# Sums for a seven-product block scheme moved to GpSimd, a ring of six tiles for the split operands, and one reordered visit

## The chip, the cores and the metric

The kernel runs on one core of a Trainium2 chip. The core has five engines that run side by side, each with its own queue of instructions taken in order: TensorE (PE, the matrix products), VectorE (DVE), ScalarE (ACT), GpSimd (POOL) and SyncE (SP, which here issues nearly all transfers). They meet at semaphores: an instruction waits at the head of its queue until what it needs is done. The metric is the device time of one execution in microseconds (us). Several executions are timed, and the median counts.

## The reference

Two things are computed one behind the other. For each of 8 batches and 8 heads, rows `x` (512 x 64) and a small state (32 x 64) attend to each other:

```python
scores = scale * x @ state.T;   a  = softmax(scores);  xread = a @ state
scores2 = scale * state @ x.T;  a2 = softmax(scores2); sread = a2 @ x
```

`xread` and `sread` of all heads make 4608 rows of 512 numbers (544 rows per batch). Each row then goes through a two-layer network with an activation that is x times the tanh of the softplus of x, called mish:

```python
h = x @ w_in                    # 512 -> 2048
g = h * np.tanh(softplus(h))
out = g @ w_out                 # 2048 -> 512
```

All is in float32.

## The kernel before

**Precision.** TensorE is run in a fast format (fp32r) that keeps fewer bits. So each operand of a large product is split in a high part (a rounded copy, `gh`) and a low part (what is left, `gl = g - gh`), and a product is three matmuls: high by high, high by low, low by high. For `g` a "unit" goes through the same steps each time: mish on ACT writes `u` (or `g`), a copy makes the high part, and a subtraction on DVE makes the low part. Then PE uses both.

**First product.** `xread` is never formed. As `xread @ w_in = a @ (state @ w_in)`, the kernel multiplies the state by a slice of `w_in` on PE (`sw_slice`, L567, output `swp`), splits the result on ACT and DVE (`swh`, `swl`), and multiplies it by the split soft-max (`ah`, `al`) in `gemm1` (L614, output `ph`). The columns of `w_in` are taken in 8 slots (`SLOTS`) of 256.

**Second product.** Batches 0 and 1 use the plain product (`second`, `gemm2`, output `acc`). From batch 2 on, blocks are multiplied by a scheme that takes seven products in place of eight: a pair of 128-row blocks by a pair of 256-column blocks, for five of the eight slots (`SEVEN = 5`); the three other slots take the plain four products of double width. The seven products need sums and differences of blocks, on both sides. Those of `w_out` are made once per slot by `seven_weights` (L891), in batch 1, slots 3 to 7. Those of `g` are made for each unit in `prepare` (L1050), in a tile `sums`, and split like `u` itself. A unit is one pair of row blocks of one slot: batch `key`, half `p` (0 or 1), slot `j`. `consume` (L1076) issues the 21 matmuls of a seven-product unit, or 12 of a plain one, to four PSUM banks (`acc_one`, `acc_two`, `acc_top`, `acc_end`), and behind the fifth unit it adds two of the banks up in `sums_{key}_{p}`.

**Order.** The main loop (L1120) takes batches 2 to 6, then the state reads (`"s"`), then batch 7. In each slot it issues: `gemm1` and mish of this slot; `one()`, a unit of the second product; `around`, which is a visit to the next batch's attention (slot 3: scores, state reads, a `sw_slice`; slot 5: a `sw_slice`; slot 7: two); `other()`, a second unit; `after` (DVE and ACT work for the next batch's soft-max, and loads); and `two_next`, which makes the parts of two more units. In batch 2 the units of the first half become ready one per slot, so `other()` has nothing to issue from slot 3 on; from batch 3 on two units are used in each slot. PE takes its instructions in the order written (`InOrder`, L56 on). From batch 1 on, DVE and ACT are ordered by a planner that works with modelled times and priorities; GpSimd is in written order. Instructions can be held behind others of the same engine (`behind`).

**Buffers.** Tiles with one tag share `bufs` places. `gh` and `gl` have two places each, of 1024 columns, so the parts of at most two units exist at a time: the high copy of the next must wait until PE has used the one two before. `g` (batches 0 and 1) has one place. Small working tiles (`temp`, five places) hold `sums` and the soft-max. A `ph` bank is one of two (`ps_h`), and a `sw_slice` in slot 7 borrows both.

Of the kernel before, what the change touches and what calls it, by code (L numbers as in the profile page):

```python
# [9 lines left out]
F32 = mybir.dt.float32  # L10
F32R = mybir.dt.float32r
# [6 lines left out]
P = 128  # L18
# [62 lines left out]
def state_attention_mish_kernel(ctx, tc, x, state, w_in, w_out, out):  # L81
# [515 lines left out]
        return gh, gl  # L597

    def new_parts(key):
        return [pool.tile([P, W], F32R, tag=t, name=f"{t}_{key}") for t in ("gh", "gl")]  # L600

    def high_g(key, g, copy=None):
        gh, gl = new_parts(key)
# [5 lines left out]
        last["low"] = dve.tensor_sub(gl, g, as_f32(gh))  # L609

    def new_g(key):
        return pool.tile([P, W], F32, tag="h", name=f"g_{key}", bufs=1)

    def gemm1(b, j, aT, sw, ks=(0, 1)):  # L614
        swh, swl = sw[j]
# [275 lines left out]
    def seven_weights(j):  # L891


        if not wx:
            wx.append(const.tile([P, SEVEN, 2, 3, 256], F32R, tag="w_in", name="wx"))
        w = pool.tile([P, 4, 256], F32, tag="wt", name=f"w_sums_{j}", bufs=1)
        dve.tensor_add(
            w.rearrange("p (k e) c -> p k (e c)", k=2), as_f32(wo[j][:, :, 0]), as_f32(wo[j][:, :, 1]))
        dve.tensor_sub(w[:, 0], w[:, 0], w[:, 1])
        dve.tensor_sub(w[:, 1], w[:, 3], w[:, 1])  # L900
        dve.scalar_tensor_tensor(w[:, 3], w[:, 3], -1.0, w[:, 0], ALU.mult, ALU.subtract)
        dve.tensor_add(w[:, 2], w[:, 2], w[:, 3])
        low, high = (wo[j][:, 0, n, 256:] for n in range(2))
        act.copy(high, w[:, 0])
        dve.tensor_sub(low, w[:, 0], as_f32(high))
        low, high = (wx[0][:, j, n] for n in range(2))
        act.copy(high, w[:, 1:])
        dve.tensor_sub(low, w[:, 1:], as_f32(high))
# [51 lines left out]
    def after(key, j):  # L960


        nonlocal sn_next
        more = key + 1 < B
        if key == 1 and j < 2:
            for g in range(2 * j, 2 * j + 2):
                nc.sync.dma_start(w_in_again[:, :, g * G:(g + 1) * G], w_in_sb[:, :, g * G:(g + 1) * G])
        if key == 1 and 3 <= j < 3 + SEVEN:
            seven_weights(j - 3)
        if key == 1 and j == 0:  # L970
            prev["soft2"]()
        if key == 1 and j == 1:
            with behind("mish"):
                prev["turn"]()
        if more and j == (0 if key == 1 else 1):
            with behind("swl"):
                for c in range(NC):
                    own["x"](c)
                own["xd"](0)
        if more and j == 1:  # L980
            with behind("swl"):
                own["st"](0)
        if more and key > 1 and j == 2:
            wis[key, 2] = load_w_in_again(2)
        if not more and j == 0:
            wis[key, 2], wis[key, 3] = load_w_in_again(2), load_w_in_again(3)
        if more and j == 3:
            with behind("swh", "swl"):
                own["soft2"]()
            if key > 1:  # L990
                wis[key, 3] = load_w_in_again(3)
        if more and j == 4:
            wis[key + 1, 0] = load_w_in_again(0)
            with behind("low before", "swh", "swl"):
                own["soft1"]()
        if more and j == 5:
            wis[key + 1, 1] = load_w_in_again(1)
            with behind("mish"):
                own["turn"]()
        if key == 1 and j == 3:  # L1000
            with behind("store"):
                xss[2] = load_x(2)
        if 1 < key < B - 1 and j == 4:
            with behind("mish"):
                xss[key + 1] = load_x(key + 1)
        if key == B - 2 and j == 6:
            with behind("mish"):
                sreads_moved()
        if more and j == 7:
            own["parts"]()  # L1010
            if key + 2 < B:
                load_x_in(key + 2)
                with behind("mish"):
                    sn_next = load_state(key + 2)
        if key == B - 2 and j == 7:
            wis["s", 0] = load_w_in_again(0, "x", 1)
            wis["s", 1] = load_w_in_again(1)
            with behind("mish", "low"):
                sreads_split()
# [30 lines left out]
    def prepare():  # L1050

        if not todo or todo[0] not in made:
            return
        unit = todo.pop(0)
        key, p, j = unit
        u = made.pop(unit).rearrange("f k h t -> f (k h) t")
        hi, lo = (pool.tile([P, 7, P], F32R, tag=t, name=f"{t}_{key}_{p}_{j}") for t in ("gh", "gl"))
        n = 3 if j < SEVEN else 4
        if j < SEVEN:
            sums = temp(f"sums_{key}_{p}_{j}").rearrange("f (s t) -> f s t", s=4)  # L1060
            dve.tensor_add(sums[:, :2], u[:, 1:3], u[:, 3:].to_broadcast([P, 2, P]))
            dve.tensor_add(sums[:, 2], sums[:, 0], u[:, 2])
            dve.tensor_add(sums[:, 3], sums[:, 2], u[:, 0])
            act.copy(hi[:, :n], u[:, :n])
            act.copy(hi[:, n:], sums)
            low_g(u[:, :n], hi[:, :n], lo[:, :n])
            low_g(sums, hi[:, n:], lo[:, n:])
        else:
            dve.tensor_copy(hi[:, :n], u)
            low_g(u, hi[:, :n], lo[:, :n])  # L1070
        parts[unit] = hi, lo
        ready.append(unit)
# [3 lines left out]
    def consume():  # L1076
# [21 lines left out]
        if j == SEVEN - 1:  # L1098
            e = spans[key, p]["sums"] = pool.tile([P, 4, 256], F32, tag="wt", name=f"sums_{key}_{p}", bufs=1)
            one, two = (banks[n].rearrange("t (h e) -> t h e", h=2) for n in ("one", "two"))  # L1100
            act.copy(e[:, 0], one[:, 0])
            dve.tensor_add(e[:, 3], e[:, 0], one[:, 1])
            dve.tensor_add(e[:, 1:3], two, e[:, 3:].to_broadcast([P, 2, 256]))
            dve.tensor_add(e[:, 3], e[:, 1], two[:, 1])

# [14 lines left out]
    for key in [*range(2, B - 1), "s", B - 1]:  # L1120
        for j in range(4 if key == "s" else SLOTS):
            one, other = halves()
            if key == "s":
                if j == 0:
                    one()
                    sread_transposed()
                    other()
                for r in range(2):
                    gemm1_s(j, r, wis["s", j], new_unit("s", 0, 2 * j + r))
                    if j:  # L1130
                        (one, other)[r]()
                if j < 2:
                    wis["s", j + 2] = load_w_in_again(j + 2, *(() if j else ("x", 1)))
            else:
                mish_units(key, j, gemm1(key, j, aTs[key], sw))
                one()
                around(key, j)
                other()
                after(key, j)
            two_next()  # L1140
# [29 lines left out]
```

## Time and profile before

| | |
|---|---|
| median of 3 runs | 662.51 us (661.88 to 664.02) |
| profiled execution | 661.25 us |
| its span in the profile | 659.5 us |
| busy in the span: PE, DVE, ACT, POOL | 633.3, 461.9, 333.3, 0.7 us |

The span is what the profile covers, from the first to the last instruction; the profiled execution's own time is 1.75 us longer. Busy time of PE counts a matmul from its start to its end, and matmuls overlap: one with 256 columns follows the one before it after some 0.12 us and one with 512 after 0.23 us, though each is shown as 0.28 or 0.39 us long. In rows of the timeline the first number is the start in the span and the second the length; rows that follow one another are merged (x2, x4). In brackets stands the idle time of the engine before the row and what ended it. Nearly all instructions carry line 73, that of the helper which records them, so they are told apart by the tile that they write and read (`gl<-u,gh`).

### The profile page before, as it was taken

What the parts mean: (1) busy time and instruction counts of PE and PEld (TensorE: products, weight loads), DVE (VectorE), ACT (ScalarE), POOL (GpSimd) and SP (SyncE); (2) the same over time, 40 slices, a digit from 0 to 9 for tenths busy, and PEclk for the clock granted to TensorE, in tenths of its full rate; (3) what the DMA queues carried; (4) which work ended last, traced back from release to release, by engine and by line L of the source; (5) the groups of instructions that cost most, each with busy time, mean ns of one, the idle gap of its engine ahead of it and who ended that gap; (6) DMA issues with size and microseconds to landing.
All of it is one profiled execution on the core that took longest, in us unless ns stands there. A gap on an engine that the chain in (4) does not pass through costs nothing.

```text
span 659.5 us, 12906 instructions
## 1 busy us (share of the span) xinstructions
PE 633.3 (96%) x5108; PEld 529.1 (80%) x5108; DVE 461.9 (70%) x951; ACT 333.3 (51%) x654; POOL 0.7 (0%) x6
## 2 busy tenths in 40 slices
PE   8999999999996899999999999999999899999997
PEld 6776777786875688797978798888888689888996
DVE  6998984799549554977398746975496787546554
ACT  5998853544346433843365444734374375343320
POOL 0000000000000000000000000000000000000000
PEclk9999999999996999999999999999999999999999
DMA  8999826412633263526263254435163441301000
GB/s 321 409 343 325 296 55 196 129 32 69 191 106 125 84 168 94 200 73 166 67 204 118 84 148 149 136 100 160 26 223 101 154 136 51 109 1 33 1 33 32
DMA packets 69035, 89.83 MB, mean 136 GB/s; under 512 B 13808, under 2 KB 42224, under 8 KB 68976
## 3 DMA queue, kind: packets, MB, share of 16 engines
q1 hardware_dynamic: 68544, 88.83, 41.9%
q8 instruction: 40, 0.66, 0.4%
q10 hardware_dynamic: 432, 0.20, 0.1%
q14 instruction: 19, 0.16, 0.1%
HBM read 63.90 MB, written 13.11 MB: 117 GB/s over the span
## 4 chain that ended last, share of the span: by engine, by line
PE 77%; DVE 10%; DMA 6%; ACT 4%; issue 2%; SPq 1%; DVEq 0%; ACTq 0%
PE ph L73 23%; PE acc_top L73 12%; PE acc L73 9%; PE acc_end L73 9%; PE acc_two L73 6%; PE acc_one L73 6%; DMA wir<-in_moe_w_in_dram 3%; PE swp L73 3%; PE ph_s L73 3%; DVE gl L73 2%; DVE sums L73 2%; DVE swl L73 1%; DMA wor<-in_moe_w_out_dram 1%; PE srp L73 1%; PE sc L73 1%
## 5 line engine op out<-in xcount | busy, mean ns | idle before, releaser
L73 ACT ACTIVATE u<-ph 128x256 f32<-128x256 f32 x192 | 63.7, 384 | 107.8 <-PE ph L73 104.0
L73 DVE TENSOR_TENSOR gl<-u,gh 128x384 fp32r<-128x384 f32 (+1 forms) x96 | 58.1, 606 | 73.7 <-ACT gh L73 72.1
L73 PE MATMUL acc_top<-wo,gh 128*128 128x256 f32 (+1 forms) x384 | 91.8, 327 | 1.0 <-DVE gh L73 1.0
L73 PE MATMUL ph<-ah,swh 128*128 128x512 f32 (+1 forms) x260 | 82.1, 396 | 8.6 <-DVE swl L73 6.4
L73 PE MATMUL ph<-ah,swl 128*128 128x512 f32 (+1 forms) x260 | 80.4, 390 | 0.0
L73 PE MATMUL ph<-al,swh 128*128 128x512 f32 (+1 forms) x260 | 80.1, 390 | 0.2 <-DVE al L73 0.2
L73 PE MATMUL acc<-wo,gh 128*128 128x512 f32 x256 | 80.0, 393 | 0.0
L73 PEld LDWEIGHTS acc_top<-wo,gh 128*128 128x128 f32 x384 | 64.0, 192 | 9.4 <-DVE srds L73 1.6
L73 ACT CAST gh<-u 128x384 fp32r<-128x384 f32 x60 | 30.9, 515 | 74.5 <-PE acc_end L73 69.0
L73 PEld LDWEIGHTS ph<-ah,swh 128*128 128x128 f32 x260 | 46.5, 189 | 22.2 <-DVE swl L73 8.6
L73 PE MATMUL acc_top<-wo,gl 128*128 128x256 f32 (+1 forms) x192 | 62.4, 325 | 0.5 <-DVE gl L73 0.5
L73 PEld LDWEIGHTS ph<-ah,swl 128*128 128x128 f32 x260 | 48.9, 189 | 11.7 <-DVE swl L73 1.2
L73 PEld LDWEIGHTS acc<-wo,gh 128*128 128x128 f32 x256 | 47.4, 188 | 12.7 <-issue 2.9
L73 PEld LDWEIGHTS ph<-al,swh 128*128 128x128 f32 x260 | 48.8, 189 | 10.9 <-DVE al L73 0.4
L73 ACT ACT_TABLE_LOAD x35 | 44.9, 1283 | 13.8 <-DVE nm L73 7.0
L73 PE MATMUL acc<-wo,gl 128*128 128x512 f32 x128 | 49.9, 390 | 0.0
L73 DVE TENSOR_TENSOR swl<-swp,swh 128x512 fp32r<-128x512 f32 (+1 forms) x72 | 42.2, 628 | 10.5 <-ACT swh L73 10.4
L73 ACT CAST swh<-swp 128x512 fp32r<-128x512 f32 (+1 forms) x72 | 34.6, 546 | 19.3 <-PE swp L73 18.7
L73 PE MATMUL acc_end<-wo,gh 128*128 128x512 f32 x144 | 44.4, 389 | 0.0
L73 DVE TENSOR_TENSOR gl<-sums,gh 128x512 fp32r<-128x512 f32 x60 | 41.5, 691 | 0.0
L73 PEld LDWEIGHTS acc_top<-wo,gl 128*128 128x128 f32 x192 | 36.8, 192 | 3.8 <-DVE gl L73 0.9
L73 ACT CAST gh<-sums 128x512 fp32r<-128x512 f32 x60 | 37.1, 618 | 4.2 <-DVE sums L73 4.2
(174 smaller groups left out, 1179.7 us busy)
## 6 DMA issues: line engine op xcount, KB each, us to landing
w_in<-w_in_again SPq DMA_DIRECT2D x28, 1024.0 KB, 6.3
x<-in_x_dram SPq DMA_DIRECT2D x32, 256.0 KB, 6.2
wir<-in_moe_w_in_dram SPq DMA_DIRECT2D x16, 512.0 KB, 10.2
wor<-in_moe_w_out_dram SPq DMA_DIRECT2D x16, 512.0 KB, 9.3
out_dram<-o SPq DMA_DIRECT2D x31, 256.0 KB, 2.6
x_rows<-x_turned SPq DMA_DIRECT2D x56, 128.0 KB, 2.4
x_in<-in_x_dram SPq DMA_DIRECT2D x24, 256.0 KB, 4.0
w_in_again<-w_in_sb SPq DMA_DIRECT2D x4, 1024.0 KB, 9.4
```

What stands on the lines that cost most here:

```text
L73: made = method(*args, **kwargs)
```

## The change

Three parts of the kernel are edited.

- `g`, `gh` and `gl`, and the two parts of a unit, all take places in one ring with the tag `"g"`, six places of 1024 columns, where there were two, two and one. A unit's parts are views of 7 x 128 columns of them.
- The sums of `w_out` blocks (five instructions for each of five slots) and the sums of `g` blocks (three for each seven-product unit) go from DVE to GpSimd. One instruction of the weights, which negated and subtracted in one step, becomes a plain addition; the sign is taken back by two subtractions, the last of the weights' five and one where the banks are added up in `consume`. `seven_weights` is now held behind the last `swl` (on DVE) and the last mish (on ACT).
- In slot 5, the sixth, `around` comes ahead of `one()`.

```diff
     def new_parts(key):
-        return [pool.tile([P, W], F32R, tag=t, name=f"{t}_{key}") for t in ("gh", "gl")]
+        return [pool.tile([P, W], F32R, tag="g", name=f"{t}_{key}", bufs=6) for t in ("gh", "gl")]
...
     def new_g(key):
-        return pool.tile([P, W], F32, tag="h", name=f"g_{key}", bufs=1)
+        return pool.tile([P, W], F32, tag="g", name=f"g_{key}", bufs=6)
...
         w = pool.tile([P, 4, 256], F32, tag="wt", name=f"w_sums_{j}", bufs=1)
-        dve.tensor_add(
+        pool_e.tensor_add(
             w.rearrange("p (k e) c -> p k (e c)", k=2), as_f32(wo[j][:, :, 0]), as_f32(wo[j][:, :, 1]))
-        dve.tensor_sub(w[:, 0], w[:, 0], w[:, 1])
-        dve.tensor_sub(w[:, 1], w[:, 3], w[:, 1])
-        dve.scalar_tensor_tensor(w[:, 3], w[:, 3], -1.0, w[:, 0], ALU.mult, ALU.subtract)
-        dve.tensor_add(w[:, 2], w[:, 2], w[:, 3])
+        pool_e.tensor_sub(w[:, 0], w[:, 0], w[:, 1])
+        pool_e.tensor_sub(w[:, 1], w[:, 3], w[:, 1])
+        pool_e.tensor_add(w[:, 3], w[:, 3], w[:, 0])
+        pool_e.tensor_sub(w[:, 2], w[:, 2], w[:, 3])
...
         if key == 1 and 3 <= j < 3 + SEVEN:
-            seven_weights(j - 3)
+            with behind("swl", "mish"):
+                seven_weights(j - 3)
...
-        hi, lo = (pool.tile([P, 7, P], F32R, tag=t, name=f"{t}_{key}_{p}_{j}") for t in ("gh", "gl"))
+        hi, lo = (
+            pool.tile([P, W], F32R, tag="g", name=f"{t}_{key}_{p}_{j}", bufs=6).rearrange("f (s t) -> f s t", t=P)
+            for t in ("gh", "gl"))
...
-            dve.tensor_add(sums[:, :2], u[:, 1:3], u[:, 3:].to_broadcast([P, 2, P]))
-            dve.tensor_add(sums[:, 2], sums[:, 0], u[:, 2])
-            dve.tensor_add(sums[:, 3], sums[:, 2], u[:, 0])
+            pool_e.tensor_add(sums[:, :2], u[:, 1:3], u[:, 3:].to_broadcast([P, 2, P]))
+            pool_e.tensor_add(sums[:, 2], sums[:, 0], u[:, 2])
+            pool_e.tensor_add(sums[:, 3], sums[:, 2], u[:, 0])
             act.copy(hi[:, :n], u[:, :n])
-            act.copy(hi[:, n:], sums)
+            act.copy(hi[:, n:7], sums)
             low_g(u[:, :n], hi[:, :n], lo[:, :n])
-            low_g(sums, hi[:, n:], lo[:, n:])
+            low_g(sums, hi[:, n:7], lo[:, n:7])
...
             act.copy(e[:, 0], one[:, 0])
-            dve.tensor_add(e[:, 3], e[:, 0], one[:, 1])
+            dve.tensor_sub(e[:, 3], e[:, 0], one[:, 1])
...
                 mish_units(key, j, gemm1(key, j, aTs[key], sw))
-                one()
+                if j != 5:
+                    one()
                 around(key, j)
+                if j == 5:
+                    one()
                 other()
                 after(key, j)
```

## The prediction

> **What bounds the kernel now.** I read the page first: the busy times, then the chain that ended last.
>
> ```profile
> span 659.5 us, 12906 instructions
> ...
> PE 633.3 (96%) x5108; PEld 529.1 (80%) x5108; DVE 461.9 (70%) x951; ACT 333.3 (51%) x654; POOL 0.7 (0%) x6
> ...
> PE 77%; DVE 10%; DMA 6%; ACT 4%; issue 2%; SPq 1%; DVEq 0%; ACTq 0%
> ```
>
> TensorE (PE) is the bound, and GpSimd (POOL) is empty. The change takes no matmul away, so it can only win time in which PE stands still: 659.5 - 633.3 = 26.2 us. The table of waits for PE, from 150 us on, says what it stood still for (total, times, longest):
>
> ```profile
> PE ph L73 <- DVE swl L73: 6.4, 5, 2.7
> PE acc_one L73 <- ACT gh L73: 4.7, 1, 4.7
> PE acc_one L73 <- DVE gl L73: 3.5, 5, 1.5
> ...
> PE acc_top L73 <- DVE gh L73: 1.0, 1, 1.0
> ```
>
> PE's timeline puts each at its place (start, length, what; in brackets the idle time before it):
>
> ```profile
> 159.99 0.73 PE L73 MATMUL ph<-ah,swh 128*128 128x512 f32 x2 [1.54 <-DVE swl L73]
> ...
> 201.81 0.79 PE L73 MATMUL acc_one<-wx,gh 128*128 128x256 f32 x2 [4.73 <-ACT gh L73]
> 204.08 0.58 PE L73 MATMUL acc_one<-wx,gl 128*128 128x256 f32 x1 [1.48 <-DVE gl L73]
> ...
> 215.74 0.98 PE L73 MATMUL ph<-ah,swh 128*128 128x512 f32 x2 [0.73 <-ACT swh L73]
> ...
> 231.74 0.73 PE L73 MATMUL ph<-ah,swh 128*128 128x512 f32 x2 [2.68 <-DVE swl L73]
> ...
> 276.26 0.39 PE L73 MATMUL acc_one<-wx,gl 128*128 128x256 f32 x1 [0.49 <-DVE gl L73]
> ...
> 300.88 0.73 PE L73 MATMUL ph<-ah,swh 128*128 128x512 f32 x2 [0.72 <-DVE swl L73]
> ```
>
> The counts of the waits follow from these. 6.4 us in five waits on swl is 1.54 + 2.68 + three of 0.72 (300.88 comes back with each batch, 72 us apart); 3.5 us in five waits on gl is 1.48 + four of 0.49 (276.26 and its like). Last, the busy time and clock by stretch (columns: PE, PEld, DVE, ACT, POOL busy, granted clock, DMA share, GB/s):
>
> ```profile
> 197.00:204.00 7.00, 0.87 (x3) 0.50 (x2) 6.24 (x17) 6.93 (x13) 0.00 (x0) 0.67 0.77 275
> 204.00:208.00 4.00, 3.92 (x17) 3.91 (x18) 4.00 (x13) 2.12 (x3) 0.00 (x0) 0.50 0.23 60
> 208.00:210.00 2.00, 2.00 (x7) 1.54 (x6) 2.00 (x6) 0.00 (x0) 0.00 (x0) 0.60 0.15 36
> 210.00:213.00 3.00, 3.00 (x22) 2.76 (x21) 2.24 (x9) 1.70 (x5) 0.00 (x0) 1.00 0.17 44
> ...
> 262.00:286.00 24.00, 23.51 (x155) 19.67 (x154) 23.94 (x61) 17.41 (x34) 0.00 (x0) 1.00 0.61 198
> ```
>
> The standstill at 197 has a second price. Behind it PE runs at half clock from 204 on; the mean of 0.60 in 208 to 210 is 1.6 us at half and 0.4 at full, so it lasts to 209.6. That is 5.6 us, which lose 2.8. The pause of 2.68 us at 231.74 is not followed by such a stretch, so the point lies between 2.7 and 4.7 us. The last row shows where VectorE (DVE) is full: 23.94 of 24 us in slots 3 to 6 of batch 3.
>
> **The change part by part.** *Sums of g on GpSimd.* Each of the 60 seven-product units of the batches (and five of the state reads) has three sums on DVE; POOL has done nothing of the kind, its nearest row is a one-input pass over 128x128:
>
> ```profile
> L73 DVE TENSOR_TENSOR sums<-u 128x256 f32<-128x256 f32 x60 | 24.4, 421 | 8.0 <-ACT u L73 7.8
> L73 DVE TENSOR_TENSOR sums<-sums,u 128x128 f32<-128x128 f32 x120 | 31.8, 287 | 0.6
> ```
>
> ```profile
> masks.py:199 POOL TENSOR_SCALAR_AFFINE_SELECT ident<-ident 128x128 f32<-128x128 f32 x1 | 0.3, 294 | 0.1
> ```
>
> DVE gives up 421 + 2 x 287 = 995 ns of busy time a unit, about 0.75 us from start to start, as instructions overlap by some 0.08. On POOL the lower bound is the same 1.0 us (128 elements in 294 ns against DVE's 287); the upper one is twice the one-input pass per element, as both inputs are read: 4 x 2 x 0.294 = 2.4 us. I take 1.4, nearer the lower row. The chain from u to the low parts is then 0.65 us longer for a unit, but no longer queues on a full DVE. The Trainium skill, GPSIMD Engine Reference, section "3.1 Elementwise — side-by-side cycle accounting", gives about 2.6 cycles per element for a two-input add; by it 512 elements at 1.2 GHz would be an estimated 1.1 us plus dispatch. No run here shows that yet, and the sum would not change.
>
> *Third pair of parts.* gh and gl had two tiles each and g one. Six in one ring hold three pairs, so a unit's parts need no longer wait until PE has used the second unit before:
>
> ```profile
> ACT gh L73 <- PE acc_end L73: 69.0, 49, 6.7
> ...
> ACT g L73 <- DVE gl L73: 14.3, 5, 5.2
> ```
>
> ```profile
> 275.52 0.69 DVE L73 TENSOR_TENSOR gl<-sums,gh 128x512 fp32r<-128x512 f32 x1
> ```
>
> In batches 0 and 1 the ring gives g a second tile, and ACT's 14.3 us of waits for it go, but none of PE's pauses above is on g; I cost it at nothing. Most of the 69 us of waits by ScalarE (ACT) go as well, which costs PE nothing by itself, but gives each unit the length of one more unit, about 2.7 us, of lead. What is late next is DVE, which is why the two edits belong together. The wait of 0.49 us at 276.26 is on that gl at 275.52, in the full stretch. It goes three times over: the lead, 0.75 us for each of its two units off DVE, and the move below. With 0.2 us of overlap that a stopped PE loses on restarting, four times: **2.8 us**. The 1.0 us on gh (the first unit behind batch 6) has the same cause in part: **0.8**.
>
> *Sixth slot's visit first.* The slot's w_in x state product (swp, 1.1 us) goes ahead of the first second-product. In batch 2 only one second-product follows, so swh at 215.74 was waited for 0.73 us; now a unit of 2.7 us lies between. The matmul pair there takes 0.98 instead of 0.73 or less, so **1.1 us**. The product needs its slice of w_in:
>
> ```profile
> 263.51 0.52 SPq L564 DMA_DIRECT2D w_in<-w_in_again  x1
> ```
>
> ```profile
> w_in<-w_in_again SPq DMA_DIRECT2D x28, 1024.0 KB, 6.3
> ```
>
> It lands at about 270, and the moved product starts at about 275. No DMA changes place. Batch 7 has nothing in that visit.
>
> *Batch boundary (swl).* A bank of ph comes free when swl has read it; DVE reaches that late:
>
> ```profile
> 158.11 1.22 DVE L73 TENSOR_TENSOR w_sums<-wo 128x1024 f32<-128x1024 f32 x1
> ...
> 229.19 0.69 DVE L73 TENSOR_TENSOR sums<-sums,u 128x128 f32<-128x128 f32 x3
> 229.80 2.48 DVE L73 TENSOR_TENSOR swl<-swp,swh 128x512 fp32r<-128x512 f32 x4
> ...
> 298.74 1.29 DVE L73 TENSOR_TENSOR swl<-swp,swh 128x512 fp32r<-128x512 f32 x2
> ...
> 300.13 1.29 DVE L73 TENSOR_TENSOR swl<-swp,swh 128x512 fp32r<-128x512 f32 x2
> ```
>
> ```profile
> 228.29 2.06 ACT L73 CAST swh<-swp 128x512 fp32r<-128x512 f32 x4 [0.27 <-PE swp L73]
> ...
> 296.44 2.06 ACT L73 CAST swh<-swp 128x512 fp32r<-128x512 f32 x4 [1.62 <-PE swp L73]
> ```
>
> At 300.13 PE waits for the first of the second pair. The window from 295 to 300 holds five sums of u, some 1.4 us; without them the second pair can begin at about 298.7, behind swh (298.5), and 0.72 goes, three times with restart: **2.7 us**. At 229.80 six sums, about 1.4 us, go; swh has its first piece by 228.9 and lets DVE start 0.9 earlier: with restart **1.0**. At 159.99 w_sums stood between the two pairs: **1.1**.
>
> *Weight sums on GpSimd.* DVE gives up 1.2 + 4 x 0.42 us for each of five slots.
>
> ```profile
> L73 DVE TENSOR_TENSOR w_sums<-w_sums x15: 382/424/433, 98.0 to 166.9; 128x256 f32<-128x256 f32 x15
> ...
> L73 DVE TENSOR_TENSOR wx<-w_sums,wx x5: 949/958/959, 124.1 to 168.3; 128x768 fp32r<-128x768 f32 x5
> ```
>
> ```profile
> 211.31 0.40 PE L73 MATMUL acc_one<-wo,gh 128*128 128x256 f32 x2
> ```
>
> On POOL the 1024 + 4 x 256 elements are 16 of its 128-element rows, 4.7 us, or 9.4 with two reads. That cover is large: the last wx is done at 169 now, and first used in the unit at 211. Only if the five ran over by more than 40 us in all would PE wait. I cost it at nothing. Behind these sums on POOL's queue stand the first units' sums, and no DMA.
>
> *The standstill at 197.* The sums of that unit end on DVE at 201.03, behind soft-max work, and gh<-sums is put behind ACT's exponentials:
>
> ```profile
> 200.78 0.25 DVE L73 TENSOR_TENSOR sums<-sums,u 128x128 f32<-128x128 f32 x1
> ```
>
> ```profile
> 198.68 0.19 ACT L73 ACTIVATION_READ_ACCUMULATOR e<-scs,nm 128x1 f32 x1
> ...
> 201.12 0.63 ACT L73 CAST gh<-sums 128x512 fp32r<-128x512 f32 x1
> ```
>
> With POOL free they can be done long before. If gh<-sums comes right behind the exponentials, at 198.9, it ends at 199.5, and gl at about 200.3: 3.1 us of idle are left of 6.2, in two parts, and the clock most likely stays (2.8 more). The bounds are 0, if ACT's order stays, and 6.2 + 2.8 = 9.0. I take **5.0**.
>
> *New waits.* ACT waits for POOL before gh<-sums, with the mish of the next slot behind it; in batch 2 units are used one slot after they are made, so the 0.65 us longer chain can show. Five units at 0.5: **-2.4**. From batch 3 on the third pair covers it.
>
> Sum: 2.8 + 0.8 + 1.1 + 2.7 + 1.0 + 1.1 + 5.0 - 2.4 = **12.1 us**. The first 150 us (PE full or waiting for loads) and the tail from 624 us (PE without a pause) stay.
>
> **Rivals.** (1) ACT's order at 197 stays, and the half clock with it: 7.1 us are won, 655.4. For it: the order is made by a planner, and soft-max was asked for earlier. (2) GpSimd holds DVE up, and it ends **slower**. The place is the full stretch from 262 to 286, with seven units' sums. If DVE stands still while POOL works, each unit costs DVE POOL's time instead of 0.75. Lead and moved product cover 2.7 + 1.1 = 3.8 us in all, so it decides from 0.75 + 3.8 / 7 = 1.3 us a unit if all of POOL's time is excluded. At 1.8 us PE would lose 7 x 1.05 - 3.8 = 3.6 us in each of batches 3 to 6, 14 us, and only the first batches' gains of about 5 would stay: 671. Against it: gl, with both inputs in SBUF, holds DVE a part of the time only, and swl, reductions, transposes have one or PSUM. The Trainium skill, SBUF — State Buffer, section "Who interferes with whom", says just this: a VectorE instruction with two SBUF inputs and a GpSimd instruction that reads SBUF exclude one another for their whole length. With POOL idle no row here can show it. (3) The waits only move, from DVE's queue to ACT's, which then stands at gh<-sums: the gains of the boundaries are eaten, about 662.
>
> **How the numbers follow.** The profiled execution took 661.25 us; the median of the runs is 662.51, 1.26 above it. 661.25 - 12.1 + 1.26 = **650.4**. Forecast 0.56 (its own range 643 to 654), rival 1 0.20, rival 2 0.14, rival 3 0.10. So faster 0.76, within 0.3% (about what a measurement here can tell from no change) 0.10, slower 0.14. The range, 643 to 665, leaves out most of rival 2 and a little below.
>
> **What would show it.** Right: the 0.49 and 0.72 us waits are gone from PE's table, no half clock behind 197, ACT's 69 us on acc_end mostly gone, POOL's three sums near 1.4 us a unit. Wrong: gl<-sums much longer than 0.69 us (exclusion), PE waiting on gh<-sums in many units (rival 3), or a new half-clock stretch. A planner that orders ACT and DVE differently everywhere could also bring waits that no row of before shows.

## The result, and the profile after

The changed kernel takes 667.88 us (median of 4 runs, 666.66 to 668.79) where the kernel before took 662.88 beside it: a ratio of 1.0074, with a 95% interval of 1.0049 to 1.0099. It is slower by 0.7%; the prediction said 650.4 us, faster, with 643 to 665 as its range.

The span and the busy times on the page of the changed kernel:

```profile
span 667.0 us, 12927 instructions
...
PE 637.2 (96%) x5108; PEld 533.4 (80%) x5108; DVE 427.0 (64%) x731; ACT 331.2 (50%) x654; POOL 165.3 (25%) x226
```

DVE is relieved by 35 us, and the span is 7.5 us longer. PE is shown busy for 3.9 us more with the same 5108 matmuls, so some of them run slower. The table of PE's waits from 150 us on (total, times, longest):

```profile
PE ph L73 <- DVE swl L73: 8.7, 2, 4.9
PE swp L73 <- DVE srds L73: 6.1, 1, 6.1
PE acc_one L73 <- ACT gh L73: 4.7, 1, 4.7
PE acc_one L73 <- DVE gl L73: 1.6, 1, 1.6
...
```

Five waits on swl have become two and five on gl one: all the short ones of 0.49 and 0.72 us are gone. Those that are left are long, and one of 0.73 us on swh, at 199.10, is as before; the other, which stood at 215.74, is gone. PE's timeline puts each at its place, and has the last `sw_slice` pair of batches 3 and 4 as a clock for the full batches (start, length, and idle time before the row):

```profile
163.82 1.22 PE L73 MATMUL ph<-ah,swh 128*128 128x512 f32 x2 [4.88 <-DVE swl L73]
...
207.48 0.79 PE L73 MATMUL acc_one<-wx,gh 128*128 128x256 f32 x2 [4.73 <-ACT gh L73]
...
237.70 1.22 PE L73 MATMUL ph<-ah,swh 128*128 128x512 f32 x2 [3.86 <-DVE swl L73]
...
302.78 1.96 PE L73 MATMUL swp<-w_in,bd 64*32 64x256 f32 x64
...
372.76 1.96 PE L73 MATMUL swp<-w_in,bd 64*32 64x256 f32 x64
...
521.74 1.95 PE L73 MATMUL swp<-w_in,bd 64*32 64x256 f32 x30 [6.12 <-DVE srds L73]
```

The same rows of the kernel before:

```profile
295.26 1.96 PE L73 MATMUL swp<-w_in,bd 64*32 64x256 f32 x64
...
367.11 1.96 PE L73 MATMUL swp<-w_in,bd 64*32 64x256 f32 x64
...
513.96 1.09 PE L73 MATMUL swp<-w_in,bd 64*32 64x256 f32 x30 [0.42 <-DVE srds L73]
```

A full batch takes 372.76 - 302.78 = 70.0 us in place of 71.85. Against that stand four **seams**, places where one stage hands over to the next, named here by the letters A, C, E and H:

| seam | idle before | idle after |
|---|---|---|
| A, first product of batch 2 | 1.54 | 4.88 |
| C, the unit of slot 4 of batch 2 | 4.73 and 1.48 | 4.73 and 1.55 |
| E, first product of batch 3 | 2.68 | 3.86 |
| H, the w_in product behind batch 6 | 0.42 | 6.12 |

A, E and H also lose clock now: in 5 to 7 us behind each of them the clock was granted in full before. The windows right behind them, and the full batches (columns as in the prediction; the clock is the first number behind POOL's):

```profile
163.80:168.80 5.00, 4.97 (x14) 3.96 (x15) 5.00 (x9) 0.75 (x3) 0.00 (x0) 0.60 0.01 1
...
237.70:243.10 5.40, 5.40 (x13) 4.27 (x14) 3.27 (x6) 0.66 (x2) 0.00 (x0) 0.52 0.30 85
521.70:529.00 7.30, 7.26 (x48) 5.13 (x49) 5.32 (x8) 4.08 (x7) 0.00 (x0) 0.69 0.48 175
```

Lost there: 5.0 x 0.40 + 5.4 x 0.48 + 7.3 x 0.31 = 6.9 us. The longer pauses cost 3.34 + 1.18 + 5.70 = 10.2. Together 17.1; as the span grew by 7.5, the change won 9.6 us elsewhere. So the question is what made A, E and H worse.

**A.** ACT, DVE and POOL between batches 1 and 2, from the three timelines of the changed kernel:

```profile
158.99 0.41 ACT L73 CAST wo<-w_sums 128x256 fp32r<-128x256 f32 x1 [3.13 <-POOL w_sums L73]
159.30 1.07 ACT L73 CAST swh<-swp 128x512 fp32r<-128x512 f32 x2
161.73 0.83 ACT L73 CAST wx<-w_sums 128x768 fp32r<-128x768 f32 x1 [1.36 <-POOL w_sums L73]
162.47 1.07 ACT L73 CAST swh<-swp 128x512 fp32r<-128x512 f32 x2
```

```profile
155.47 4.03 DVE L73 TENSOR_TENSOR al<-at,ah 128x512 fp32r<-128x512 f32 x2
159.91 1.29 DVE L73 TENSOR_TENSOR swl<-swp,swh 128x512 fp32r<-128x512 f32 x2 [0.41 <-ACT swh L73]
```

```profile
154.92 2.90 POOL L73 TENSOR_TENSOR w_sums<-wo 128x1024 f32<-128x1024 f32 x1 [1.94 <-DVE wx L73]
```

ACT takes its queue in order: both copies of swh stand behind copies of the weights' sums, which wait for POOL. Before, swh was one row of four:

```profile
155.91 2.04 ACT L73 CAST swh<-swp 128x512 fp32r<-128x512 f32 x4
```

On DVE, the two subtractions of al took 4.03 us beside POOL's 2.90 us sum (1.29 us for two such at 226.05 before); swl, which reads one operand from PSUM, keeps its 1.29 us beside POOL's next four sums, which last until 161.7.

**E.** DVE ahead of the first product of batch 3:

```profile
232.03 1.09 DVE L73 TENSOR_TENSOR gl<-u,gh 128x384 fp32r<-128x384 f32 x1
233.05 0.94 DVE L73 TENSOR_TENSOR gl<-sums,gh 128x512 fp32r<-128x512 f32 x1
233.92 0.80 DVE L73 TENSOR_TENSOR gl<-u,gh 128x384 fp32r<-128x384 f32 x1
234.65 1.21 DVE L73 TENSOR_TENSOR gl<-sums,gh 128x512 fp32r<-128x512 f32 x1
235.78 2.47 DVE L73 TENSOR_TENSOR swl<-swp,swh 128x512 fp32r<-128x512 f32 x4
```

The low parts of two units stand ahead of swl, and they are longer than the 556 and 691 ns that such subtractions took on average before (the runs below show which of the two counts).

**H.** `sr_turned` holds the turned state reads of the first seven batches, and 16 transfers carry it to `sr_moved`. ACT's row behind batch 6, after and then before, and the transfers (SP's queue) that it waits for, also after and then before:

```profile
518.51 0.37 ACT L73 COPY sums<-acc_one 128x256 f32<-128x256 f32 x1 [6.12 <-DMA sr_moved<-sr_turned]
```

```profile
510.73 0.37 ACT L73 COPY sums<-acc_one 128x256 f32<-128x256 f32 x1 [0.42 <-DMA sr_moved<-sr_turned]
```

```profile
505.70 11.49 SPq L544 DMA_DIRECT2D sr_moved<-sr_turned  x16
```

```profile
498.71 10.70 SPq L544 DMA_DIRECT2D sr_moved<-sr_turned  x16
```

sums_{key}_{p} (L1102) and sr_turned (L538) share the one place of the tag "wt". The copy waits until 16 transfers have read it, and these started 7.0 us later in the span. PE's own work up to there was only 2.1 us later (7.8 us at H less the 5.7 of longer pause).

### The profile page after: what moved, and what is told of

It is laid out like the page before. It is cut to its first block, busy times and chain, and to the rows that moved or that the text cites. A ratio compares the mean times of both kernels' runs of the same rounds, so it can differ in the third digit from the quotient of the medians.

```text
span 667.0 us, 12927 instructions
## 1 busy us (share of the span) xinstructions
PE 637.2 (96%) x5108; PEld 533.4 (80%) x5108; DVE 427.0 (64%) x731; ACT 331.2 (50%) x654; POOL 165.3 (25%) x226
## 4 chain that ended last, share of the span: by engine, by line
PE 75%; DMA 8%; DVE 6%; SPq 3%; POOL 3%; ACT 2%; issue 1%; DVEq 0%; ACTq 0%
PE ph L73 22%; PE acc_top L73 13%; PE acc_end L73 10%; PE acc L73 6%; PE acc_two L73 6%; PE acc_one L73 6%; PE swp L73 4%; DMA wir<-in_moe_w_in_dram 3%; PE ph_s L73 3%; POOL w_sums L73 3%; DMA x<-in_x_dram 2%; DMA wor<-in_moe_w_out_dram 2%; SPq L544 1%; DVE gl L73 1%; PE acc_s_top L73 1%
## 5 line engine op out<-in xcount | busy, mean ns | idle before, releaser
L73 POOL TENSOR_TENSOR sums<-u 128x256 f32<-128x256 f32 x60 | 53.6, 893 | 310.8 <-DVE u L73 81.0
L73 DVE TENSOR_TENSOR gl<-u,gh 128x384 fp32r<-128x384 f32 (+1 forms) x96 | 62.7, 653 | 62.6 <-ACT gh L73 59.6
L73 PE MATMUL ph<-ah,swh 128*128 128x512 f32 (+1 forms) x260 | 83.3, 402 | 10.2 <-DVE swl L73 8.7
L73 PE MATMUL ph<-al,swh 128*128 128x512 f32 (+1 forms) x260 | 81.5, 396 | 0.2 <-DVE al L73 0.2
L73 POOL TENSOR_TENSOR sums<-sums,u 128x128 f32<-128x128 f32 x120 | 70.3, 586 | 9.4
L73 DVE TENSOR_TENSOR gl<-sums,gh 128x512 fp32r<-128x512 f32 x60 | 48.4, 807 | 4.8 <-ACT gh L73 4.7
L73 DVE CAST gh<-u 128x512 fp32r<-128x512 f32 x36 | 16.8, 466 | 49.1 <-PE acc_end L73 39.2
L73 POOL TENSOR_TENSOR w_sums<-wo 128x1024 f32<-128x1024 f32 x5 | 13.8, 2759 | 126.2 <-DVE wo L73 92.3
```

What stands on the lines that cost most here:

```text
L73: made = method(*args, **kwargs)
```

## The experiments

The times are medians, the ratios are to the kernel before on the same chip. Seams are in the letters above.

**The weights' sums back on DVE.** The hold of `seven_weights` stays.

```diff
-        pool_e.tensor_add(w.rearrange(...), ...)
+        dve.tensor_add(w.rearrange(...), ...)
...
-        pool_e.tensor_sub / tensor_add (four)
+        dve.tensor_sub / tensor_add (four)
```

> The changed kernel with the five weight sums per slot back on VectorE, nothing else. Theory: the pause of 4.88 us in front of batch 2 (at 163.82) and the half clock behind it come from ScalarE, whose casts of w_out sums stand at the head of its queue until GpSimd has made the sums (9.8 us of waits on POOL w_sums), with swh and so swl behind them. Then the pause falls to 1.5 us or less, PE stays at full clock there, and the time falls by 3.4 + 2.0 = 5.4 us, to about 662.5. Rival: the low parts that the third pair lets in ahead of swl make the pause; then it stays near 4.9 and the time at 667 to 668.

665.88 us, 1.0048 (1.0033 to 1.0064). Pause A only went from 4.88 to 3.94 us, and the half clock behind it stayed; the 662.5 us expected were missed, and so was the rival's pause of 4.9. By the pause POOL's slowness is 0.9 us of A; the whole time is 2 us less than the changed kernel's, which the intervals of the two don't separate. Most of A has another cause.

**The sums of g back on DVE.** Ring, visit and the weights' sums on GpSimd stay.

```diff
-            pool_e.tensor_add(sums[:, :2], ...)   # and two more
+            dve.tensor_add(sums[:, :2], ...)      # and two more
```

> The changed kernel with the sums of g blocks back on VectorE; ring, visit and weight sums on GpSimd as in the change. Theory: the third pair carries the gain of the full batches, so their period stays near 70.0 us (71.9 before); VectorE's instructions with two inputs in SBUF go back to their 0.69 us, the pause of 3.86 us in front of batch 3 falls to about 2.7 and loses its half clock, 3.6 us, and the state reads' wait of 6.1 us shrinks by some us: 660 to 664. Rival: taking the sums off VectorE carried the gain; then the period goes back to 71.9, PE waits on gl and swl come back in each batch, and the time is 667 to 671.

670.84 us, 1.0112 (1.0084 to 1.0141): 3 us more than the whole change, though the intervals overlap a little. In PE's timeline the waits of 0.72 us came back, at 309 us and twice more, 71.0 us apart:

```profile
309.09 0.73 PE L73 MATMUL ph<-ah,swh 128*128 128x512 f32 x2 [0.72 <-DVE swl L73]
```

A full batch takes 71.0 us here and 70.0 in the changed kernel. So the offload of these sums is worth its price, and the price POOL puts on DVE does not decide. E is 3.74 us here too, with POOL out of DVE's way there: exclusion isn't what made E longer.

**sr_turned out of the shared place,** into the ring.

```diff
-        u = pool.tile([P, 4, B - 1, NS], F32, tag="wt", name="sr_turned", bufs=1)
+        u = pool.tile([P, W], F32, tag="g", name="sr_turned", bufs=6)[:, :4 * (B - 1) * NS].rearrange(
+            "p (s b n) -> p s b n", s=4, b=B - 1)
```

> The changed kernel with the turned state reads (sr_turned) in a place of the ring of six, where they shared the one place of the tag wt with the sums of two banks. Theory: the 6.12 us for which PE waited on srds is the copy of bank one that cannot have its tile until sixteen transfers have read sr_turned; then that wait is under 0.5 us, no half clock follows, and the time falls by 6.1 + 1.4 = 7.5 us, to about 660.4. Rival: with one place of the ring gone PE waits for gh or gl of the plain units there instead, or the transfers themselves are needed then; the time stays above 665.

662.78 us, 0.9994 (0.9982 to 1.0005): 5.1 us of the loss are gone with this line, of the 7.5 expected. Where 6.12 us were waited for srds, 1.85 us are left, at the transpose of the last state reads (srTp), with full clock behind them. H is shown to be the shared place.

**The parts ahead of the soft-max in slot 3 of batch 2.**

```diff
                 other()
+                if key == 2 and j == 3:
+                    two_next()
                 after(key, j)
-            two_next()
+            if key != 2 or j != 3:
+                two_next()
```

> The changed kernel with the parts of the next units asked for ahead of the soft-max work in slot 3 of batch 2 alone. Theory: the pause of 4.73 + 1.55 us at 207 is an order: the unit's sums take their small working tile behind the two exponentials, so ScalarE's copy of them is planned behind the exponentials and a table load, although GpSimd had them 11 us before. Then pause and half clock go, 6.3 + 2.8 us less the 0.7 of swh that stays, and the time is about 659. Rival: the soft-max of the next batch is what is late there; then it only moves, PE waits as long for another tile of the same stretch, and the time is 666 to 668.

665.92 us, 1.0053 (1.0035 to 1.0071). C, its 4.73 and 1.55 us, is gone, and a new pause stands one slot later, with a half clock behind it (0.50 over 5.5 us):

```profile
216.56 1.28 PE L73 MATMUL ph<-ah,swh 128*128 128x512 f32 x2 [4.00 <-ACT swh L73]
```

```profile
213.43 0.66 ACT L73 ACTIVATE u<-ph 128x256 f32<-128x256 f32 x2
214.11 1.28 ACT L73 ACT_TABLE_LOAD   x1
215.40 0.63 ACT L73 ACTIVATE e<-e 128x512 f32<-128x512 f32 x1
215.94 1.05 ACT L73 CAST swh<-swp 128x512 fp32r<-128x512 f32 x2
```

The planner now takes exponentials of the second soft-max and mish in turn, with a table load of 1.28 us at each change, and swh stands behind them. C is ACT's order, as the theory said; the order of the next slot ate the gain.

**The ring undone.** Two places each for gh and gl and one for g; the rest of the change stays.

```diff
-tag="g", name=..., bufs=6      # g, gh, gl and the two parts
+tag="h" / tag="gh" / tag="gl"  # one, two and two places
```

> The changed kernel with the ring undone: gh and gl have two places each and g one, as before; sums on GpSimd and the moved visit stay. Theory: the 0.49 us waits on gl in batches 3 to 6 come back where the pair of places binds (in the earlier run with the sums on VectorE and the ring kept they stayed away), the boundary of batches 2 and 3 falls from 3.86 us back to 2.7 or less, since only one unit's two subtractions can stand ahead of swl there, and sr_turned still stands where the ring does not touch it (6.12 us stays). Sum against the changed kernel: about -2.5 at the boundary with its half clock, +2 for the returned waits: 667.5, within 1.5 of the changed kernel. Rival: the lengthening of that boundary is GpSimd's exclusion of VectorE alone (its subtractions took 0.8 to 1.2 us there): then it stays at 3.5 us or more, and the time is 669 to 670. Second rival: with two places ScalarE's order in batch 1 is also as before, and the pause at 164 us falls from 4.88 to 2 us or less: then about 664.

662.81 us, 0.9994 (0.9976 to 1.0011): 5 us better than with the ring, and better than any of the three cases expected. E fell to 2.36 us, with no half clock, as expected; only one unit's two subtractions stand ahead of swl. A fell to 3.17 us and H to 3.95, both with a half clock still behind them. Against that, the place of g is one again and PE waited for g in batch 1, 1.68 us at 142.64, which it does not with the ring. The returned 0.49 us waits, which the expectation counted, did not come: so the third pair was not what took them away.

**The weights as before:** on DVE, and no longer held.

```diff
-            with behind("swl", "mish"):
-                seven_weights(j - 3)
+            seven_weights(j - 3)
```

> The changed kernel with the sums of w_out on VectorE, as in the earlier run, and in addition seven_weights no longer held behind the last swl and the last mish; the ring, the sums of g on GpSimd and the moved visit stay. Theory: what was left of the pause at 164 us in that earlier run (3.94 us and a half clock) is the hold, which pushes the weights' copies and sums of batch 1's last slots into the stretch where swh and swl of the boundary are due; without the hold the pause is 1.54 us as before the change, with no half clock, and the time falls from 665.9 by 2.4 us of idle and 2.5 us of half clock to about 661. Rival: it is the ring (g has more places, so ScalarE and VectorE run ahead with other work in batch 1): then the pause stays at 3 us or more and the time at 665 to 666.

662.25 us, 0.9978 (0.9963 to 0.9992). PE's timeline:

```profile
159.68 0.74 PE L73 MATMUL ph<-ah,swh 128*128 128x512 f32 x2 [1.62 <-DVE swl L73]
```

A is back at 1.62 us with full clock, though the ring is still there. So most of A was the hold (3.6 us of time between this run and the first of the experiments), and the ring makes no such pause by itself; E, 3.87 us, is untouched. No run has the sums on POOL without the hold, so what POOL's time alone would cost at A isn't shown.

**The ring alone,** put into the kernel before.

```diff
-tag="h" / tag=t                # g; gh, gl and the two parts
+tag="g", name=..., bufs=6
```

> The kernel before with the ring of six alone: all sums on VectorE, the visit where it was, the weights without a hold. Theory: the third pair of parts alone takes the four 0.49 us waits away (about -2.8 with restarts, as the sum of the prediction had it), and costs what goes wrong at the places that depend on it: the boundary of batches 2 and 3 becomes 3.7 us with a half clock (+1 and +2.5); the pause at 160 us stays at 1.5 us. Together 663, within 1.5 of the kernel before. Rival: the ring with the shorter queue of no offload makes VectorE late in more places, as the returned 0.72 us waits with the sums on VectorE suggest, and the state reads' wait behind batch 6 grows: then 665 to 668. Second rival: the boundary is lengthened only by the GpSimd sums: then 659 to 661.

667.16 us, 1.0061 (1.0042 to 1.0081): slower, by 4.1 us, as the first rival had it. E is 3.68 us with nothing on POOL at all:

```profile
233.23 0.94 PE L73 MATMUL ph<-ah,swh 128*128 128x512 f32 x2 [3.68 <-DVE swl L73]
...
298.73 1.96 PE L73 MATMUL swp<-w_in,bd 64*32 64x256 f32 x64
...
370.96 1.96 PE L73 MATMUL swp<-w_in,bd 64*32 64x256 f32 x64
```

A full batch takes 72.2 us, no shorter than before, and behind batch 6 there are 2.47 us on srds. So by itself the third pair brings nothing in the full batches and costs at E and H.

**Only the offload and the visit,** with each seam's cause undone: no ring, weights as before, and sr_turned in its own place (without the ring there is room for one).

```diff
-        u = pool.tile([P, 4, B - 1, NS], F32, tag="wt", name="sr_turned", bufs=1)
+        u = pool.tile([P, 4, B - 1, NS], F32, tag="sr", name="sr_turned", bufs=1)
```

> Of the change only the g sums on GpSimd and the moved visit are kept: the ring is undone (two places each for gh and gl, one for g), the sums of w_out are on VectorE without a hold, and sr_turned has a place of its own, for which there is room without the ring. Theory: each of the four seams is set by one part that is gone here, so the pauses are 1.6 us at the boundary of batches 1 and 2, 2.4 at that of 2 and 3 without half clock, and 1.9 or less in place of the 4 to 6 us wait on srds behind batch 6; the standstill near 200 us stays at 4.7 + 1.6 with its half clock; the 0.49 and 0.72 us waits stay away. From the run with the ring undone (662.8): -1.6 and -2.1 to -4: 657 to 659, faster than the kernel before. Rival: the planner finds other orders, and a pause of 3 us or more comes at another place: 661 or more.

655.32 us, 0.9887 (0.9859 to 0.9915): faster than the kernel before and than the changed one, by more than expected. A is 1.54, E 2.01 with full clock, H 0.31 us; C is as it was. At E the two gl rows took 0.82 and 0.94 us (0.56 and 0.69 before): so a part of the forecast gain there was lost beside POOL. A full batch takes 70.0 us without the ring:

```profile
292.23 1.96 PE L73 MATMUL swp<-w_in,bd 64*32 64x256 f32 x64
...
362.26 1.96 PE L73 MATMUL swp<-w_in,bd 64*32 64x256 f32 x64
```

Behind batch 6 PE still waits 1.62 us for gh, and the clock in the 5.8 us behind that is 0.71. The run with the ring and sr_turned in it has no such wait; there the third pair may help, but no run separates it.

**The same, and parts held behind swl** in the last slot of batch 2.

```diff
-            two_next()
+            with behind(*(("swl",) if key == 2 and j == 7 else ())):
+                two_next()
```

> The same, and in the last slot of batch 2 the parts of the next two units are held behind the last swl. Theory: at that boundary the parts' subtractions stand ahead of swl on VectorE; behind it they cost nothing, since the units are used later: 2.4 us becomes 1.5 or less, and the time falls by 1 us against the kernel without the hold. Rival: swl is late because swh is late behind ScalarE's work, so the hold changes nothing there (2.4 us stays) and the parts come later than the first unit needs them: then it is up to 2 us slower.

659.17 us, 0.9934 (0.9910 to 0.9958), and its runs lie far apart (653.82 to 661.55). swl is the first row on DVE now, but has to wait for swh: the pause went from 2.01 to only 1.79 us, and 1.74 us on gl came a little later. That is what the rival said, though the loss of 3.9 us is larger than its 2. The rest stands behind batch 6: 1.55 us at srTp in place of 0.43, with a clock of 0.58 from 516 to 524 us.

**The second soft-max a slot later.** The kernel of 655.32 us with the parts first in slot 3, and `soft1` of batch 2 (the soft-max that is asked for second) in slot 5.

```diff
+                if key == 2 and j == 3:
+                    two_next()
                 after(key, j)
-            two_next()
+            if key != 2 or j != 3:
+                two_next()
...
-        if more and j == 4:
+        if more and j == (5 if key == 2 else 4):
             with behind("low before", "swh", "swl"):
                 own["soft1"]()
```

> The kernel with the offload and the visit alone, and in batch 2 two moves: in slot 3 the parts are asked for ahead of the soft-max of the state reads, and the other soft-max (soft1) is asked for in slot 5 in place of slot 4. Theory: the standstill near 200 us is ScalarE's planned order. gh<-sums is planned behind the exponentials since they were asked for first; asking for the parts first took the 4.7 + 1.6 us away in the earlier run and left a pause of 4 us at the next slot, where the second soft-max with its table loads (1.28 us each) came between mish and swh. With that soft-max one slot later both are gone, no half clock is left between 197 and 217 us, and the time falls by 6.3 + 2.8 = up to 9 us against the kernel without the moves; 5 or more means the theory holds. Rival: the soft-max finds no place in slot 5 either and its exponentials hold up swh or the parts of slot 6 or 7: then a pause of 3 us or more shows between 218 and 235 us and the gain is under 3 us.

652.32 us, 0.9837 (0.9810 to 0.9864). Between 195 and 219.7 us the clock is full, and no pause of over 0.3 us is left: C is gone and did not come back a slot later. But E grew:

```profile
224.95 1.22 PE L73 MATMUL ph<-ah,swh 128*128 128x512 f32 x2 [5.25 <-DVE swl L73]
```

The moved soft-max now ends close to E, and al and the parts stand ahead of swl. Behind E the clock is 0.50 for 5.4 us. 3 us were won of the 9 that C held, much as the rival said (a pause of 3 us or more there, a gain under 3).

**The soft-max cut in two:** only its exponentials and what follows go to slot 5, and the parts are held behind swl in slot 7.

```diff
-                own["soft1"]()
+                own["soft1" if key != 2 else "soft1_first"]()
         if more and j == 5:
+            if key == 2:
+                with behind("swh"):
+                    own["soft1_rest"]()
...
-                two_next()
+                with behind(*(("swl",) if key == 2 and j == 7 else ())):
+                    two_next()
```

> The kernel with the offload, the visit and the parts of slot 3 ahead of the soft-max, and two more moves in batch 2: of soft1 only the exponentials and what follows them are asked for in slot 5, its transposes and maxima in slot 4 as before; and in slot 7 the parts of the next two units are held behind the last swl. Theory: the 5.25 us before the first product of batch 3, left in the run before, are VectorE's queue ahead of swl: soft1's end came late (the exponentials began at 212.2 us, waiting for VectorE), and the parts' two subtractions (0.8 and 1.2 us) stood between al and swl. With the exponentials right behind swh of slot 5 and the parts behind swl the pause is 2.5 us or less, without a half clock: from 652.3 to 647 to 649. Rival: the parts, now behind swl, come too late for the first units of batch 3 (as the 1.74 us on gl in the run with the hold alone), with a half clock: 651 or more.

**649.0 us**, 0.9798 (0.9774 to 0.9821), 13.4 us less than the kernel before and the shortest of all. The time is that of the theory, and so is the pause; but the rival's wait on gl came as well, and a shorter half clock behind it (0.81 from 226 to 235 us):

```profile
221.81 0.73 PE L73 MATMUL ph<-ah,swh 128*128 128x512 f32 x2 [1.79 <-DVE swl L73]
227.14 0.50 PE L73 MATMUL acc_top<-wo,gl 128*128 128x512 f32 x1 [1.85 <-DVE gl L73]
```

What each of the two moves gave isn't separated.

**The visit undone** in the kernel of 655.32 us, so that only the sums of g on GpSimd (and sr_turned's place) are left.

```diff
-                if j != 5:
-                    one()
+                one()
                 around(key, j)
-                if j == 5:
-                    one()
```

> The kernel with the offload and the visit alone (655.3 us, ring undone, sums of w_out on VectorE, sr_turned in its own place), with the visit undone: of the change only the sums of g on GpSimd are left. Theory: the visit is what takes the 0.73 us wait on swh in slot 6 of batch 2 away and a part of the 0.49 us waits on gl; without it the 0.73 comes back, and at least some of the 0.49s: 1 to 3.5 us slower, 656.5 to 659. Rival: the shorter queue of VectorE alone takes the 0.49 us waits away and the visit is worth only the 0.73: within 1.2 us of 655.3.

660.47 us, 0.9963 (0.9944 to 0.9982): the visit is worth 5.1 us there, more than either theory had. A full batch takes 70.7 us without the visit. The 0.7 us stand in slot 6, between two matmuls, where the table of waits shows nothing: at 282.86 us two matmuls with swl take 1.10 us in place of 0.62, and they start 0.24 us later than matmuls that follow one another. Most likely PE has caught up with DVE there; the same two matmuls in the ring alone (1.10 us at 286.03) do wait for swl, 0.35 us, but in this run no wait is recorded. The rest is the 0.73 us on swh in batch 2, 1.6 us at srTp (2.03 for 0.43), and a half clock of 1.7 us behind E (see the last section). With four times 0.7 that makes 6.8 us; the two profiled executions lie 6.7 apart.

## Why the prediction was wrong

*Full batches, 0.49 and 0.72 us waits (gain of 5.5).* **Right in size, a little short:** 71.85 to 70.0 us a batch, 7.4 us in batches 3 to 6. The reason was half right. The offload took the 0.72s away (they came back without it), and offload and visit together did the rest. The third pair, to which the prediction gave the lead, had no part: without it a batch takes 70.0 us as well, and with it alone 72.2. That the size came out is partly luck. ACT's wait on acc_end, 69.0 us before and forecast to be mostly gone, is still there, in ACT's table of waits:

```profile
ACT gh L73 <- PE acc_end L73: 61.3, 39, 3.9
...
ACT gh L73 <- POOL sums L73: 6.5, 6, 1.5
```

*The price of a unit on POOL.* Taken as 1.4 us, which was too small; groups of instructions of the changed kernel, by form:

```profile
L73 POOL TENSOR_TENSOR sums<-sums,u 128x128 f32<-128x128 f32 x120 | 70.3, 586 | 9.4
L73 POOL TENSOR_TENSOR sums<-u 128x256 f32<-128x256 f32 x60 | 53.6, 893 | 310.8 <-DVE u L73 81.0 <-DVE gl L73 81.0 <-ACT u L73 62.7
...
L73 DVE TENSOR_TENSOR gl<-sums,gh 128x512 fp32r<-128x512 f32 x60 | 48.4, 807 | 4.8 <-ACT gh L73 4.7
```

0.89 + 2 x 0.59 = 2.07 us, near the upper bound. That is beyond the 1.3 us of rival 2, and yet PE did not wait in the full batches. Rival 2 let DVE stand still for all of POOL's time, but a unit's two gl rows became only 0.18 us longer together (807 and 618 ns, before 691 and 556). The Trainium skill, SBUF — State Buffer, section "Who interferes with whom", says that a VectorE instruction with two SBUF inputs contends with a GpSimd instruction that reads SBUF. The rows at A agree with it: al, with two SBUF inputs, took 4.03 us, and swl, with one in PSUM, its usual 1.29. Two inputs aren't the whole of it: DVE's rounding copies, with a single input, were longer too (gh<-u of 128x512 466 ns, before 423; gh<-g of 128x1024 781, before 685), while its reductions and transposes of 128x512 kept their 0.67 to 0.71 us.

*Weight sums on GpSimd "at nothing".* **This step failed.** It compared the last wx (169 us) with its first use (211) and took 40 us of cover. The work also sits in queues: with the hold, the copies of two slots' sums came into the stretch where swh and swl of batch 2's start are due, and stood ahead of them on ACT. With the forecast gain of 1.1 not made either, A cost 3.3 us of idle and 2.0 of clock. Taken back one after the other, POOL's part was 0.9 us of the pause (2 us of time, within the noise) and the hold's 2.3 us with the half clock, 3.6 us of time. The hold stands in the diff, and the prediction put no price on it.

*Third pair, a gain without a price.* **This step failed too.** The prediction gave it the lead and no term for a cost. It lets the parts of two units, not one, be made at the end of batch 2, so four subtractions stand ahead of swl at E. Instead of the forecast gain of 1.0 at that boundary, 1.2 us of idle and 2.6 of clock were lost. Undoing the ring gave 5 us in all, at E, A and H and less what came back in batch 1. There the prediction took g's second place at nothing; with one place and the hold PE did wait for g.

*Behind batch 6 (gain of 0.8).* **This step failed as well:** it had a gain and no cost. The wait on gh went, but 5.7 us of idle and 2.3 of clock came at H. The prediction did not look at which places the end of batch 6 shares. The row that warned was in the profile of before (ACT's at 510.73): ACT waited there 0.42 us for sr_moved, so the transfers had no slack, and anything that delayed them had its price on PE. They were 7 us later; each of ring (2.47 us by itself) and the rest of the change (3.95 without the ring) lengthened H. A part of the delay can be read: `sr_moved` has its place in common with the tile from which the transfers of e2T read (tag "sc", L394 and L541), and SP's queue waits 2.8 us for the last of these, where it waited 0.3 before; these 16 transfers go out until 502.4 us in place of 497.4, and the transposes that feed them start at 486.59 on DVE in place of 483.77. Why they are late stays open.

*The standstill at 197 (gain of 5.0).* Rival 1 came true here in full. POOL had the sums at 195.3 us; ACT took them up at 206.80:

```profile
193.28 0.74 POOL L73 TENSOR_TENSOR sums<-u 128x256 f32<-128x256 f32 x1 [5.47 <-ACT u L73]
194.10 1.23 POOL L73 TENSOR_TENSOR sums<-sums,u 128x128 f32<-128x128 f32 x2
```

```profile
206.80 0.63 ACT L73 CAST gh<-sums 128x512 fp32r<-128x512 f32 x1
```

The faster input did nothing, since the planner had put the copy behind the exponentials. The runs that moved the request instead of the work removed C; what they won in all depended on where the soft-max went.

*Visit (1.1).* Right for its place, as the 0.73 us at 215.74 are gone, and too small: 5.1 us in the kernel without ring and hold, of which 0.7 us a batch, srTp and the half clock behind E were not in this term.

*New waits (-2.4).* The changed kernel shows nothing of this term on PE (five units at 0.5 are 2.5, not 2.4). ACT did wait for POOL's sums (the second row of its waits above, 6.5 us in six waits), but PE's table has no new wait on gh: its one of 4.7 us is C, where the sums were ready 11 us before. The loss came at the seams, to which the prediction gave only gains. The nearest of its cases is rival 3, waits that move to ACT, but at A alone and not at gh<-sums.

## What to carry to other kernels

When work moves to another engine or a ring gets longer, look at each place where a stage begins and ask what now stands ahead of its first operands in each in-order queue; an average that improves by 2 us a batch is easily eaten there, the more so if a pause brings a half clock. A buffer's place that two unrelated tiles share is such a queue too, and a wait of 0.4 us on it in the old profile meant that it had no slack. An input made earlier helps only if its consumer is also planned earlier.

## What the runs showed of the hardware

*Half clock and the length of a pause.* The prediction put the point between 2.7 and 4.7 us. Windows of 5 us right behind E, in the kernel with the visit undone (a pause of 2.00 us) and in the one with the visit (2.01):

```profile
230.50:235.50 5.00, 4.94 (x15) 3.92 (x16) 3.54 (x7) 0.95 (x4) 0.28 (x1) 0.66 0.53 158
```

```profile
229.50:234.50 5.00, 4.92 (x22) 4.07 (x23) 3.98 (x8) 1.32 (x4) 0.29 (x1) 1.00 0.48 141
```

The same pause cost 1.7 us of clock in one and none in the other, and a pause of 2.68 us in the kernel before cost none. So the length of a pause alone doesn't decide. The Trainium skill, TensorE: Matmul & The Clock Gate, section "What's actually happening", speaks of a free-running window of about 3.4 us, which would make it a matter of phase. That agrees with two outcomes for one length, but 2.00 us of idle is less than such a window, so by that figure one pause of idle time can't be all that is counted here. What else is, stays open.

*GpSimd.* A sum of 128x256 took 0.74 us with DVE nearly idle (at 193.28 in the changed kernel) and 0.89 on average; one of 128x1024 took 2.90 at A, beside al. The prediction's estimate from the Trainium skill, GPSIMD Engine Reference, section "3.1 Elementwise — side-by-side cycle accounting", was 1.1 us plus dispatch for a unit's three sums. They take 0.74 + 1.23 = 1.97 us at that place; that the difference is dispatch is not shown.
